# Key rows of a block in the order own 64, next 32, and a new listed order of all engines

## The chip, the cores and the metric

The kernel runs on one core of a Trainium2 chip. The metric is the time of one execution in microseconds, as the device reports it; for each version the median of several runs is given. The span of a profile runs from the first to the last instruction and is a little shorter than that time.

## The reference

Block-sparse attention with a window, then a two-layer network. Four batches, eight heads, 768 positions, head size 64.

```python
# attention: block, window = 32, 16
k_sum = k.reshape(B, H, nb, block, D).max(axis=3)          # 24 block keys
v_sum = v.reshape(B, H, nb, block, D).mean(axis=3)         # 24 block values
scores_l = scale * (q @ k.T), kept where |i - j| < 16
scores_s = scale * (q @ k_sum.T) + log(32)
a = softmax(concat[scores_l, scores_s])                    # over 768 + 24 columns
attn = a @ concat[v, v_sum]
# network on x = attn as [3072, 512]
h = x @ w_in                                               # 512 -> 2048
out = (h * clip(h + 3, 0, 6) / 6) @ w_out                  # 2048 -> 512
```

## The kernel before

**Attention.** A batch's 768 queries are cut into 12 blocks of 64, shifted by 16 rows against the blocks of keys. A block of queries needs 96 key rows (`WIN`) and the 24 block maxima, so that a block's scores are one product of 120 rows (`KEYS`). `kaug[p]` holds the keys so arranged for pair p of heads, `vaug[i]` the values (batch b in `vaug[b % 2]`). Of the 96 rows of block t, rows 0 to 31 are the last 32 of block t - 1 and rows 32 to 95 the 64 of block t itself. The first block wraps around; a mask kills what does not belong. The queries of block t start 16 rows before 64 t, so the query tile `qT` begins with 16 wrapped rows.

Values arrive by `load_v` in rows 32 to 95; the rows of the block before are copied on the chip (`halo`, batches 0 and 1) or loaded a second time (`load_ahead` and the copy "round", batches 2 and 3). The block sums of the values (`vsum_first`, `vsum`) are products with an indicator `ind` over all 96 rows, in which the first 32 rows of the indicator are zero. Those rows must hold numbers, so `empty` fills them with zeros once for each of two tiles and four pairs, and halos and sums wait for that.

Each batch is worked off in two halves of six blocks. Half 0 is the upper half of the positions (`low(x)` is `(1 - x) * HQ`), because block 0 is the one that wraps around. A half of a batch is one stage s of the network, s = 0 to 7.

**Steps of attention, by tag.** `k`p transposes the keys of batch 0 and takes maxima, `q`g transposes queries, `w`bp turns keys and queries of batches 1 to 3 by block transposes on VectorE, `s`bph makes scores, exponentials (ScalarE) and masks (VectorE), `u`g makes block sums and spreads them, `v`bhg multiplies by values, divides by the sum and transposes to x. For s of 4 and above x is transposed by a VectorE block transpose and 16 small moves in SyncE's queue (line 649).

**The network.** F`s`x`ft` is one group of four matmuls into a bank of PSUM (line 667), a ScalarE relu (line 671) and a VectorE gate (line 672). G`s``ts`x0 accumulates 16 matmuls of 512 columns in four parts (line 684), then an output copy on ScalarE or VectorE (line 242) and a store in SyncE's queue. Of the last output tile three column slices are separate; one of them (`ofinish`, lines 698 and 699) is copied and stored by ScalarE.

**What sets the order.** The string `ORDER` lists every step; each engine executes its steps in the order of that list. `:A` and `:D` place a step that either ScalarE or VectorE can do. Dependences become waits. Buffers of PSUM (three banks "h", one "o", two pairs "S") are given out in the order of the list, the one longest free first, so that the list also fixes which step a bank waits for. Tokens such as `_40`, `-15` and `~12` are matmuls on a constant tile: 40 of 64 columns, 15 of 128, 12 of 512; `=3` is one of 192. All loads are issued by GpSimd: K, Q, V, H for keys, queries, values and next rows, I and O for the two weights. The list begins:

```python
c.0 K00.0 c.7 c.17 c.6 c.8:A K01.0 c.10:D c.5 c.1 _40 -15 k0.0 k0.2:A c.18 ~1 =2 k1.0 K02.0 ~12 =3 k2.0 k3.0 ...
```

Here `c.0` to `c.20` are the constants (`c.1` identity, `c.2` the window, `c.3` the bias, `c.4` the mask, `c.5` the indicator, `c.6` and `c.7` edges of `vaug`, `c.8` to `c.15` the zero fills, `c.17` to `c.20` edges of `kaug`). Keys of pair 0 are loaded first, those of pairs 2 and 3 (`K02`) together and last; then queries, values of pairs 0 to 3, and the wide query tiles `Q0w0` to `Q0w2` of the second half.

Of the kernel before, what the change touches and what calls it, by code (L numbers as in the profile page):

```python
# [9 lines left out]
F32 = mybir.dt.float32  # L10
BF16 = mybir.dt.bfloat16
AF = mybir.ActivationFunctionType
# [17 lines left out]
c.0 K00.0 c.7 c.17 c.6 c.8:A K01.0 c.10:D c.5 c.1 _40 -15 k0.0 k0.2:A c.18 ~1 =2 k1.0 K02.0 ~12 =3 k2.0 k3.0 c.15:D c.2 c.3  # L30
s000.0 k0.3:A c.13:D c.4 c.11:A k1.1 Q00.0 q0.0 k1.4 k0.1 c.20 k1.2:A Q01.0 ~2 =5 q1.0 k0.4 k1.3:D c.9:A c.14:A c.19 k2.3:A
q0.1:A s000.1 q0.2:A =1 s010.0 s010.1 k2.2:A k3.2:D k3.3:D k3.1 V00.0 h000.0:D h001.0:D k2.1 k2.4 s000.2 ~2 =5 v00.0 V01.0 u0.0
h010.0:D s020.0 c.16 s010.2 q1.2:A u0.3:D u0.1:D u0.4:D v01.0 v01.1 v01.2 v00.1 q1.1:A V02.0 h020.0:A h021.0:A h011.0:A v00.2
s020.1 v01.3 v00.3 V03.0 u1.0 u1.3:A h030.0:D s030.0 k3.4 ~2 s030.1 u1.4:D v01.4 h031.0:D Q0w0.0 Q0w1.0 v01.5:D Q0w2.0 =1 q3.0
q3.1:D q2.0 u1.1:A u1.2:D s020.2 v02.0 v02.1 v02.2 s021.0 v02.3 s030.2 v03.0 v03.1 q2.1:A v03.2 s011.0 v03.3 v00.4 v00.5:D
v02.4 s021.1 s011.1 s021.2 v03.4 v03.5:D s011.2 v02.5:A s031.0 s031.1 s001.0 s031.2 I2.0 F0x3.0 F0x3.1 F0x3.2 F0x3.3 F0x3.4
F0x3.5 I4.0 F0x6.0 F0x6.1 F0x6.2 F0x4.0 F0x4.1 F0x4.2 F0x4.3 v411.0 v411.1 F0x5.0 F0x4.4 F0x4.5 v411.2 s001.1 I8.0 u0.2:A
s001.2 F0x8.0 F0x8.1 F0x8.2 F0x5.1 I0.0 F0x5.2 F0x11.0 F0x1.0 F0x11.1 F0x11.2 F0x1.1 F0x1.2 F0x1.3 F0x1.4 F0x1.5 v410.0 v410.1
F0x7.0 F0x7.1 F0x7.2 v410.2 F0x10.0 F0x10.1 I12.0 F0x13.0 F0x13.1 F0x15.0 F0x15.1 F0x13.2 F0x10.2 v411.3 v411.4:D v410.3
v410.4:A F0x15.2 F0x14.0 F0x14.1 F0x14.2 F0x9.0 F0x9.1 F0x9.2 F0x0.0 F0x0.1 F0x2.0 F0x2.1 K13.0 K10.0 c.12:A F0x0.2 K12.0 K11.0  # L40
w10.0 Q1w1.0 F1x14.0 F1x14.1 F1x14.2 F1x4.0 F1x4.1 F1x4.2 F1x2.0 F1x2.1 F1x2.2 w10.1:D F0x2.2 F0x2.3 F0x2.4 F0x12.0 F0x12.1
F0x12.2 F1x8.0 F1x8.1 F1x8.2 F1x1.0 F1x1.1 F1x1.2 F0x0.3 F0x0.4 F0x0.5 F0x2.5 F1x9.0 F1x9.1 F1x9.2 F1x5.0 F1x5.1 F1x5.2 F1x15.0
F1x15.1 w11.0 w11.2 F1x15.2 w11.3:D Q1w4.0 Q1w2.0 Q1w0.0 w10.2 w10.3:D q6.0 q6.1:A q7.0 q7.1:A F1x7.0 F1x7.1 w11.1:A F1x7.2
F1x12.0 F1x12.1 F1x12.2 O0.0 G02x0.0 Q1w5.0 Q1w3.0 q4.0 q4.1:A q5.0 q5.1:A F1x6.0 F1x6.1 F1x6.2 O1.0 G02x0.1 s100.0 s100.1
s100.3 F1x3.0 w12.0 F1x11.0 F1x11.1 w13.0 w13.2 F1x3.1 F1x11.2 w12.2 w12.1:D O2.0 G02x0.2 s101.0 s101.1 O3.0 F1x10.0 G02x0.3
G02x0.4:A w13.3:D w13.1:A s101.3 F1x0.0 G00x0.0 G00x0.1 w12.3:D s100.2 s101.2 s100.4 V10.0 h100.0:D F1x10.1 h110.0:A F1x10.2
F1x3.2 s110.0 s110.1 s110.2 s101.4 s110.3 G00x0.2 G00x0.3 G00x0.4:A V12.0 u4.0 h130.0:D h120.0:A F1x0.1 u4.1:D u4.2:A u4.4:D
u4.3:D u4.5:D G02x0.5 G01x0.0 G01x0.1 G01x0.2 s110.4 F1x0.2 h111.0:A v100.0 v100.1 v100.2 h121.0:A v101.0 v101.1 v101.2 G01x0.3
G01x0.4:A K20.0 K21.0 K22.0 K30.0 K23.0 w21.0 F1x13.0 F1x13.1 F1x13.2 v100.3 v100.4:A w20.0 w21.3 G12x0.0 w21.2:A v101.3
v101.4:A V22.0 H2.0 h101.0:A w20.3 G12x0.1 G12x0.2 F2x2.0 F2x2.1 F2x11.0 F2x2.2 F2x11.1 F2x11.2 s111.0 w23.0 s111.3 F2x1.0  # L50
F2x1.1 F2x1.2 F2x3.0 F2x3.1 F2x3.2 F2x15.0 F2x15.1 F2x15.2 Q22.0 w23.3 G12x0.3 s111.1 G12x0.4:A F2x5.0 F2x5.1 h131.0:A F2x5.2
F2x6.0 G10x0.0 s111.2 w22.0 w22.3 s111.4 w23.4:A V20.0 H2.1:A K33.0 F2x13.0 F2x13.1 F2x13.2 G10x0.1 F2x6.1 F2x0.0 F2x0.1 F2x0.2
u5.0 u5.1:A u5.5:A F2x6.2 v110.0 v111.0 v111.1 v111.2 Q30.0 F2x4.0 F2x4.1 F2x4.2 Q21.0 Q23.0 Q20.0 w22.4:A F2x10.0 F2x10.1
# [109 lines left out]
def kernel(  # L163
# [80 lines left out]
    def low(x):  # L244

        return (1 - x) * HQ
# [563 lines left out]
```

## Time and profile before

| | |
|---|---|
| median of 3 runs | 216.65 us (216.47 to 217.7) |
| profiled execution: span from first to last instruction | 214.9 us |
| outside that span, median less span | 1.75 us |
| TensorE busy | 208.8 us, 97% |
| VectorE busy | 162.7 us, 76% |
| ScalarE busy | 135.9 us, 63% |
| GpSimd busy | 49.5 us, 23% |
| DMA moved | 22.68 MB |

The page gives no other time for the profiled execution than its span; the rest of its time lies before the first and after the last instruction. Engines: PE is TensorE, PEld its weight loads, DVE VectorE, ACT ScalarE, POOL GpSimd, SP SyncE. In the table of stretches a row gives from:to, the length, each engine's busy time with its instructions in brackets, the granted TensorE clock and the DMA share. In groups of instructions "busy, mean ns" stands ahead of the bar and the idle time of the engine before them behind it. A row of the chain gives its start, its length and what ran. Durations of one engine overlap, so that starts of two neighbours can lie closer than the duration of the first.

### The profile page before, as it was taken

What the parts mean: (1) busy time and instruction counts of PE and PEld (TensorE: products, weight loads), DVE (VectorE), ACT (ScalarE), POOL (GpSimd) and SP (SyncE); (2) the same over time, 40 slices, a digit from 0 to 9 for tenths busy, and PEclk for the clock granted to TensorE, in tenths of its full rate; (3) what the DMA queues carried; (4) which work ended last, traced back from release to release, by engine and by line L of the source; (5) the groups of instructions that cost most, each with busy time, mean ns of one, the idle gap of its engine ahead of it and who ended that gap; (6) DMA issues with size and microseconds to landing.
All of it is one profiled execution on the core that took longest, in us unless ns stands there. A gap on an engine that the chain in (4) does not pass through costs nothing.

```text
span 214.9 us, 6125 instructions
## 1 busy us (share of the span) xinstructions
PE 208.8 (97%) x2564; PEld 119.7 (56%) x2564; DVE 162.7 (76%) x318; ACT 135.9 (63%) x264; POOL 49.5 (23%) x66
## 2 busy tenths in 40 slices
PE   7998999999999999999999999999999999999994
PEld 7566656555555565565555555555555555564443
DVE  6987999999899999898899889887865555550021
ACT  3987878887898988756578696566346355520110
POOL 7977358906643244000000000000000000000000
PEclk9999999999999999999999999999999999999999
DMA  5999999999999999930334234113314400113123
GB/s 75 159 155 189 203 188 170 190 203 162 206 160 187 181 135 151 108 146 11 38 37 143 28 37 110 49 21 39 70 19 81 78 0 3 49 49 122 52 80 139
DMA packets 91724, 22.68 MB, mean 106 GB/s; under 512 B 82224, under 2 KB 88752, under 8 KB 91696
## 3 DMA queue, kind: packets, MB, share of 16 engines
q0 software_dynamic: 62288, 14.41, 72.7%
q1 hardware_dynamic: 29264, 7.80, 15.4%
q8 instruction: 20, 0.33, 0.6%
q10 hardware_dynamic: 144, 0.07, 0.1%
q14 instruction: 8, 0.07, 0.1%
HBM read 28.82 MB, written 6.29 MB: 163 GB/s over the span
## 4 chain that ended last, share of the span: by engine, by line
PE 86%; POOL 5%; DMA 4%; DVE 1%; ACT 1%; issue 1%; POOLq 0%
PE h L667 38%; PE o L684 33%; PE h L684 5%; DMA qwide<-in_q_dram 4%; PE S L624 3%; PE S L513 3%; POOL vaug L344 2%; PE S L554 1%; ACT vaug L242 1%; POOL first L306 1%; PE S L637 1%; POOL qwide L326 1%; PE S L440 1%; PE S L667 1%; POOL first L313 1%; PE h L582 1%
## 5 line engine op out<-in xcount | busy, mean ns | idle before, releaser
L667 PE MATMUL h<-x,win 128*128 128x384 bf16 x500 | 91.1, 326 | 0.3 <-DVE g L672 0.3
L671 ACT ACTIVATE r<-h 128x384 f32<-128x384 f32 x125 | 58.7, 492 | 38.8 <-PE h L667 36.8
L672 DVE SCALAR_TENSOR_TENSOR g<-r,h 128x384 bf16<-128x384 f32 x125 | 65.7, 546 | 22.7 <-ACT r L671 20.1
L684 PE MATMUL o<-wout,g 128*128 128x512 bf16 x336 | 81.7, 379 | 0.0
L667 PEld LDWEIGHTS <-win 128*128 128x128 bf16 x512 | 48.7, 98 | 35.9 <-issue 0.5
L684 PEld LDWEIGHTS <-g 128*128 128x128 bf16 x416 | 38.7, 98 | 37.4 <-issue 0.3
L521 ACT ACTIVATE at<-S 120x768 bf16<-120x768 f32 x24 | 18.6, 811 | 5.5 <-PE S L513 5.4
L242 ACT COPY ot<-o 128x512 f32<-128x512 f32 x17 | 10.0, 586 | 15.4 <-PE o L684 14.2
L522 DVE TENSOR_TENSOR at<-at,mask 96x768 bf16<-96x768 bf16 x24 | 12.6, 549 | 2.0 <-ACT at L521 1.6
L606 DVE TENSOR_TENSOR xn<-S,rc 128x768 bf16<-128x768 f32 x14 | 13.3, 950 | 0.3
L242 DVE COPY ot<-h 128x512 f32<-128x512 f32 (+1 forms) x3 | 1.6, 555 | 14.3 <-PE h L684 14.3
L344 POOL DMA_DIRECT2D vaug<-in_v_dram x10 | 11.8, 1191 | 0.4 <-DMA first<-in_k_dram 0.2
L684 PE MATMUL h<-wout,g 128*128 128x128 bf16 (+2 forms) x80 | 11.4, 294 | 0.0
L468 DVE TENSOR_REDUCE red<-kaug 128x24 bf16<-128x768 bf16 x12 | 11.2, 942 | 0.1
L242 ACT COPY vaug<-vaug 32x640 bf16<-32x640 bf16 (+3 forms) x17 | 8.9, 574 | 0.8 <-DMA vaug<-in_v_dram 0.5
L242 ACT COPY vaug<-vs 24x1536 bf16<-24x1536 bf16 x6 | 8.8, 1468 | 0.6 <-DVE vs L242 0.5
L456 DVE STREAM_TRANSPOSE kaug<-kraw 128x768 bf16<-128x768 bf16 x8 | 8.1, 1020 | 0.3 <-PE S L513 0.3
L778 PE MATMUL o<-idle 128*128 128x64 bf16 (+2 forms) x70 | 7.0, 278 | 1.1 <-DVE idle L288 1.1
L334 POOL DMA_DIRECT2D kraw<-in_k_dram x8 | 5.9, 737 | 8.9 <-DVE kaug L456 7.3
L513 PEld LDWEIGHTS <-kaug 32*128 32x128 bf16 x576 | 5.3, 92 | 4.4 <-issue 3.6
L643 DVE STREAM_TRANSPOSE y<-xn 128x768 bf16<-128x768 bf16 x8 | 7.6, 964 | 0.2
L624 PEld LDWEIGHTS <-at 120*64 120x64 bf16 x336 | 6.2, 111 | 2.6 <-issue 1.5
(107 smaller groups left out, 183.6 us busy)
## 6 DMA issues: line engine op xcount, KB each, us to landing
out_dram<-ot SPq DMA_DIRECT2D x19, 256.0 KB, 2.3
vaug<-in_v_dram POOLq DMA_DIRECT2D x6, 384.0 KB, 13.1
wout<-in_moe_w_out_dram POOLq DMA_DIRECT2D x4, 512.0 KB, 9.9
win<-in_moe_w_in_dram POOLq DMA_DIRECT2D x3, 512.0 KB, 10.8
kraw<-in_k_dram POOLq DMA_DIRECT2D x8, 192.0 KB, 12.9
x<-y SPq DMA_DIRECT2D x64, 24.0 KB, 2.0
first<-in_k_dram POOLq DMA_DIRECT2D x6, 192.0 KB, 12.3
first<-in_q_dram POOLq DMA_DIRECT2D x6, 192.0 KB, 12.3
```

Of the source, the lines that this page charges most:

```text
L242: {"ACT": nc.scalar.copy, "DVE": nc.vector.tensor_copy, "POOL": nc.gpsimd.tensor_copy}[eng](o, i)
L344: op("POOL", "dma128", lambda: nc.gpsimd.dma_start(out=o[BLK:WIN, a:z, 0:D], in_=rows[:, a:z]), w=[("v", b % 2, c) for c in range(lo, hi)] ...
L468: op("DVE", "max", lambda: nc.vector.tensor_reduce(red.slot[:], w[:, :, BLK:WIN].rearrange("p t (n c) -> p t n c", n=2), axis=AX.X, op=ALU ...
L513: nc.tensor.matmul(X[g // 2].slot[:, g % 2, i * QB:(i + 1) * QB], kaug[2 * u + m][rows, t], qT[rows, 2 * u + m, t * QB:(t + 1) * QB], star ...
L521: op("ACT", "exp", lambda a=a, e=e: nc.scalar.activation(a, X[e].slot[0:KEYS, :, 0:HALF], AF.Exp, scale=scl), r=[X[e]], w=[("at", p, half)])
L522: op("DVE", "masking", lambda m=m: nc.vector.tensor_tensor(m, m, mask[:, low(half):low(half) + HQ].unsqueeze(1).to_broadcast([WIN, 2, HQ, ...
L606: nc.vector.tensor_tensor(o, src[..., 0:D], r.unsqueeze(len(r.shape)).to_broadcast(list(o.shape)), op=ALU.mult)
L624: nc.tensor.matmul(X.slot[64 * c:64 * c + 64, i, m:m + D + 1], a[:, t * QB:(t + 1) * QB], vaug[b % 2][0:KEYS, h, t, 0:D + 1], start=True, ...
L667: nc.tensor.matmul(bank(h)[:, 0:HALF], w_in_sb[:, kt, cols], xt[s].slot[:, kt], start=(kt == 0), stop=(kt == NP - 1))
L671: op("ACT", "relu", lambda: nc.scalar.activation(r.slot[:], bank(h)[:, 0:HALF], AF.Relu, bias=0.5, scale=1.0 / 6.0), r=[h], w=[r])
L672: op("DVE", "gate", lambda: nc.vector.scalar_tensor_tensor(gt[s].slot[:, ft], r.slot[:], 1.0, bank(h)[:, 0:HALF], op0=ALU.min, op1=ALU.mul ...
L684: nc.tensor.matmul(o.slot[:, a:z], gt[s].slot[:, ft, ts * 128:(ts + 1) * 128], w_out_sb[:, ft, a:z], start=(ft == 0), stop=(ft == NFT - 1))
```

## The change

Key rows of block t are now its own 64 in rows 0 to 63 and the first 32 of block t + 1 in rows 64 to 95; the last block wraps around. The queries of block t start at 64 t + 16, and the 16 wrapped rows stand at the end of `qT`. Half 0 is the lower half of the positions. The block sums read rows 0 to 63 alone, so their indicator has 64 rows, the eight zero fills are gone, and neither halos nor sums wait for them or for the neighbouring rows. Wrapped stores and loads move from the first to the last tile. The list is new as a whole: its opening loads `K02` first, then both query loads, `K01`, `K00` and values 3, 2, 1, 0, and begins TensorE with 17 constant matmuls of 512 columns and 17 of 128.

```diff
-c.0 K00.0 c.7 c.17 c.6 c.8:A K01.0 c.10:D c.5 c.1 _40 -15 k0.0 k0.2:A c.18 ~1 =2 k1.0 K02.0 ~12 =3 k2.0 k3.0 c.15:D c.2 c.3
-s000.0 k0.3:A c.13:D c.4 c.11:A k1.1 Q00.0 q0.0 k1.4 k0.1 c.20 k1.2:A Q01.0 ~2 =5 q1.0 k0.4 k1.3:D c.9:A c.14:A c.19 k2.3:A
+c.0 c.6 K02.0 Q01.0 Q00.0 c.1 K01.0 ~17 -17 k2.0 K00.0 V03.0 c.9 c.12 c.10 V02.0 k3.0 k3.3:A c.11 k2.1 c.2 ~5 =2 q0.0 q1.0
+V01.0 k2.4 k3.1 k3.2:D V00.0 q0.1:D c.3 Q0w2.0 k2.2:A k3.4 ~3 s030.0 q0.2:A c.4 k0.0 q1.2:A s030.1 c.5 k2.3:A s020.0 q1.1:A
+s020.1 k1.0 h030.0:D Q0w1.0 s030.2 v03.0 k0.2:A s020.2 k1.2:A k0.1 k1.1 c.8 Q0w0.0 u1.0 k0.4 s000.0 I4.0 k1.4 I2.0 I0.0 s000.1
+u1.3:D k1.3:D u1.1:D s000.2 s010.0 h020.0:D k0.3:D h000.0:A s010.1 v03.1 u0.0 v00.0 h010.0:D v03.2 v02.0 u0.1:D v02.1 u0.3:A
+s010.2 v00.1 v03.3 v01.0 I12.0 I8.0 v02.2 v01.1 u1.2:A q3.0 q2.0 h011.0:A v00.2 v00.3 v02.3 v01.2 v00.4 K13.0 u1.4:D q3.1:D
+h031.0:A q2.1:D v01.3 v00.5:D s021.0 s001.0 v03.4 c.7 h021.0:A v02.4 v01.4 s021.1 s031.0 v03.5:D K10.0 v02.5:D F0x4.0 s001.1
+v01.5:A s021.2 K12.0 s011.0 F0x3.0 F0x3.1 F0x3.2 s031.1 K11.0 s011.1 s001.2 F0x6.0 F0x3.3 F0x1.0 Q1w1.0 F0x3.4 F0x1.1 F0x6.1
...
+F4x2.0 F4x10.1 G32x0.1 G32x0.2 F4x2.1 F4x10.2 G32x0.3 w30.2:D v211.2 F4x11.0 G32x0.4:A F4x0.2 s300.0 s300.3 v210.3 F4x3.0
+F4x2.2 G30x0.0 F4x3.1 u6.5:D G30x0.1 F4x11.1 s300.1 v211.3 s300.4 G30x0.2 u6.2:A w30.5:A w32.1 G01x0.5 F4x3.2 F4x1.0 w33.5:D
...
-G70x0.4:D G70x0.5 G60x0.0 G60x0.1 G60x0.2 G72x0.4:D G72x0.5 G60x0.3 G71x256.1 G71x256.2 G60x0.4:D G60x0.5 G71x256.3 G71x256.4
-G71x384.0 G71x384.1 G71x384.2 G71x384.3 G71x384.4:D G71x384.5
+G52x0.5 G70x0.2 G72x0.3 G71x0.0 G70x0.3 G71x0.1 G72x0.4:D G61x0.5 G72x0.5 G71x256.0 G60x0.2 G60x0.3 G71x384.5 G71x0.2 G70x0.4:A
+G71x256.1 G71x0.3 G60x0.4:D G71x0.4:D G71x256.2 G71x256.3 G71x256.4 G60x0.5 G70x0.5 G71x0.5
...
-    ind = sb([WIN, NQ, 32], BF16, "ind")
+    ind = sb([QB, NQ, 32], BF16, "ind")
...
-        return (1 - x) * HQ
+        return x * HQ
...
-    def empty(eng, i, c):
...
-        for c in range(NP):
-            op(EITHER, "empty", lambda eng, i=i, c=c: empty(eng, i, c), r=["idle"], w=[("vh", i, c)])
...
-        op("POOL", "dma128", lambda: nc.gpsimd.dma_start(out=o[BLK:WIN, a:z, 0:D], in_=rows[:, a:z]),
+        op("POOL", "dma128", lambda: nc.gpsimd.dma_start(out=o[0:QB, a:z, 0:D], in_=rows[:, a:z]),
...
-            copy(eng, o[0:BLK, hs, a:z, 0:D], o[QB:WIN, hs, a - 1:z - 1, 0:D])
+            copy(eng, o[QB:WIN, hs, a:z, 0:D], o[0:BLK, hs, a + 1:z + 1, 0:D])
...
-            out=w[:, :, BLK:WIN].rearrange("p t (r s) -> p t s r", s=2), in_=blocks_of(kraw[(b + 1) % 2][:])),
+            out=w[:, :, 0:QB].rearrange("p t (r s) -> p t s r", s=2), in_=blocks_of(kraw[(b + 1) % 2][:])),
...
-                    nc.tensor.matmul(T.slot[32 * c:32 * c + 32, 0, 0:2 * D], ind[:, t], vaug[i][0:WIN, 2 * c:2 * c + 2, t, 0:D],
+                    nc.tensor.matmul(T.slot[32 * c:32 * c + 32, 0, 0:2 * D], ind[:, t], vaug[i][0:QB, 2 * c:2 * c + 2, t, 0:D],
                                      start=(t == 0), stop=(t == NQ - 1))
-        op("PE", "sums4", mms, r=[("v", i, c) for c in range(NP)] + ([("vh", i, c) for c in range(NP)] if b == 1 else [("vh", i)]) + ["ind"], w=[T])
+        op("PE", "sums4", mms, r=[("v", i, c) for c in range(NP)] + ["ind"], w=[T])
...
-            b, row = s // 2, 128 * ((s % 2 * 3 + ts + 3) % 6) - PAD
-            n = max(-row, 0)
+            b, row = s // 2, 128 * (s % 2 * 3 + ts) + PAD
+            n = max(row + 128 - S, 0)
```

179 lines of the change are left out of this document (83 added, 96 removed).

## The prediction

> **What bounds the kernel now.** I read the page first, then the table of stretches, then the chain that ended last.
>
> ```profile
> span 214.9 us, 6125 instructions
> ```
> ```profile
> core 0: us, PE busy (x) PEld busy (x) DVE busy (x) ACT busy (x) POOL busy (x), PEclk, DMA share, GB/s
> 8.00:16.00 8.00, 7.79 (x156) 4.74 (x155) 6.98 (x22) 6.93 (x14) 6.92 (x9) 1.00 2.13 161
> 24.00:44.00 20.00, 19.70 (x228) 12.12 (x220) 18.70 (x38) 16.43 (x32) 13.32 (x16) 1.00 1.68 187
> 44.00:64.00 20.00, 19.87 (x371) 10.80 (x369) 18.60 (x37) 16.94 (x31) 9.31 (x10) 1.00 1.97 182
> 64.00:84.00 20.00, 20.00 (x251) 11.62 (x249) 19.01 (x31) 17.69 (x39) 8.26 (x9) 1.00 1.85 164
> 84.00:104.00 20.00, 20.00 (x291) 11.17 (x290) 18.46 (x33) 13.13 (x27) 0.00 (x0) 1.00 0.83 90
> 104.00:124.00 20.00, 20.00 (x237) 10.79 (x235) 17.73 (x33) 14.61 (x26) 0.00 (x0) 1.00 0.34 63
> ```
> ```profile
> 20.31 0.73 PE h L442 x10
> ...
> 24.24 2.06 PE h L667 x12
> ...
> 57.50 0.84 PE S L554 x48
> ...
> 119.52 1.73 PE o L684 x8
> 121.25 1.95 PE h L667 x12
> ...
> 210.36 1.58 PE h L684 x28
> ```
>
> From 24.2 us on TensorE has hardly a gap (19.70 and 19.87 of 20, then all of it) until its last matmul at 210.36 + 1.58 = 211.9. An F matmul costs 1.95/12 = 0.162 us, a G matmul 1.73/8 = 0.216 us, and the change alters the number of neither. So a new order can win only in the opening before 24.2 us and in the 3.0 us after 211.9; in the 187.7 us between it can only lose. Next to TensorE stands VectorE: 18.70 + 18.60 + 19.01 + 18.46 + 17.73 = 92.5 of the 100 us from 24 to 124. That is the second limit.
>
> **The parts that cost nothing.**
>
> ```profile
> L283 DVE MEMSET vaug<- 32x768 f32 x3 | 2.1, 698 | 0.4 <-issue 0.2
> L285 ACT ACTIVATE vaug<-idle 32x768 f32<-32x768 bf16 x5 | 4.1, 836 | 0.0
> L554 PE MATMUL S<-vaug,ind 96*32 96x128 bf16 x144 | 2.6, 220 | 0.0
> L513 PE MATMUL S<-qT,kaug 32*128 32x64 bf16 x576 | 6.6, 190 | 0.0
> L490 PE MATMUL S<-qT,kaug 64*128 64x64 bf16 x96 | 2.6, 191 | 0.1
> ```
> ```profile
> 2.42 0.70 DVE L283 MEMSET vaug<- 32x768 f32 x1 [0.19 <-issue]
> ...
> 4.84 0.26 DVE L262 TENSOR_SCALAR bias<-band 96x384 bf16<-96x384 bf16 x1 [0.25 <-POOL band L258]
> 5.19 0.70 DVE L283 MEMSET vaug<- 32x768 f32 x1
> 5.82 0.44 DVE L265 COPY mask<-band 96x768 bf16<-96x768 bf16 x1
> ...
> 6.63 0.96 DVE L403 TENSOR_REDUCE red<-h 128x24 bf16<-128x768 bf16 x1
> ```
>
> The eight zero fills go: 3 x 0.70 us of VectorE and 5 x 0.84 us of ScalarE. VectorE's three lie between 2.42 and 5.89, before its first reduction over keys at 6.63: it would wait for keys anyway. Four of ScalarE's five lie in the opening, where it is busy 6.93 of 8 us, and it has 11 to 34% free in every later stretch. Gain 0; its bounds are 0 and the 2.1 us of VectorE. The block sums read 64 rows and not 96 with the same five groups of matmuls (5 x 0.84 = 4.2 us). If rows set the time, a third (1.4 us) would go; but matmuls of 64 and of 32 rows take 191 and 190 ns, so I take 0. Their wait for the next-block rows goes as well; TensorE was not idle there. Wrap-around rows, their split stores and split loads move to the other end in equal number: 0.
>
> **The opening, in the new order.** Key pairs 2 and 3 come first in one load of 384 KB, then both query loads, then keys 1 and 0, then v in the order 3, 2, 1, 0.
>
> ```profile
> 1.13 3.71 PE L778 MATMUL o<-idle 128*128 128x64 bf16 x55 [1.13 <-DVE idle L288]
> ...
> 6.45 2.85 PE L778 MATMUL o<-idle 128*128 128x512 bf16 x13
> ```
> ```profile
> first<-in_k_dram POOLq DMA_DIRECT2D x1, 384.0 KB, 5.5
> ```
> ```profile
> 25.56 1.20 DVE L672 SCALAR_TENSOR_TENSOR g<-r,h 128x384 bf16<-128x384 f32 x2
> ...
> 28.92 1.48 DVE L672 SCALAR_TENSOR_TENSOR g<-r,h 128x384 bf16<-128x384 f32 x3
> ```
>
> The filler matmuls show two speeds: 40 of 64 and 15 of 128 columns, 4480 in 3.69 us, are 0.82 ns a column; thirteen of 512, 6656 in about 2.8, are 0.42. The new filler ahead of the first transpose is 17 x 512 + 17 x 128 = 10880 columns from the same 1.13 us: 4480 slow until 4.8, the other 6400 x 0.42 = 2.7 until 7.5. The 384 KB need 5.5 us from issue at 1.36, so 6.9. The first transposes (0.5 us) thus start at 7.5, and VectorE's first reduction at 8.0, where it is 6.63 now.
>
> From there to the end of its first gate (line 672, due at 25.56 + 0.55 = 26.1 now) VectorE has 40 instructions now and 43 in the new order. Counted with the mean of each kind, that is 17.9 and 20.6 us: bias (0.26), mask (0.44 and its small fills), block indicator and one edge fill, 2.1 us together, which now fill its wait for keys, come after the keys, and one masking, two query copies and a sum copy are added (1.9), against two halo copies, a spread and two fills fewer (1.3). Durations overlap: three gates of 0.546 take 1.48, a ratio of 0.90; with the waits between engines I take 0.93. So 8.0 + 20.6 x 0.93 = 27.2: the first gate is 1.1 us late. Up to the gate of F0x15 follow 12 gates, two reciprocals, two scalings, a copy and a transpose, 10.5 x 0.93 = 9.8, until 37.0 us. By then TensorE has run as many F groups as by the same time before (16 of s = 0 but one, two of s = 1), because before it was itself the limit, at 0.65 us a group. Walked on bank by bank, the first block sum of batch 1 starts near 56.5, now 57.50, with 0.9 us more matmuls behind it. I take 0 for the opening, between -1.5 (VectorE at ratio 0.86) and +1.6.
>
> **VectorE after the opening.** The order hands copies from ScalarE to VectorE: nine of twelve spreads of block sums (now six), ten output copies (now seven), three wide query copies (now one); two third-row copies and two spreads of maxima go the other way.
>
> ```profile
> L672 DVE SCALAR_TENSOR_TENSOR g<-r,h 128x384 bf16<-128x384 f32 x125 | 65.7, 546 | 22.7 <-ACT r L671 20.1
> L522 DVE TENSOR_TENSOR at<-at,mask 96x768 bf16<-96x768 bf16 x24 | 12.6, 549 | 2.0 <-ACT at L521 1.6
> L606 DVE TENSOR_TENSOR xn<-S,rc 128x768 bf16<-128x768 f32 x14 | 13.3, 950 | 0.3
> L468 DVE TENSOR_REDUCE red<-kaug 128x24 bf16<-128x768 bf16 x12 | 11.2, 942 | 0.1
> L456 DVE STREAM_TRANSPOSE kaug<-kraw 128x768 bf16<-128x768 bf16 x8 | 8.1, 1020 | 0.3 <-PE S L513 0.3
> ```
>
> F4x6 reuses the bank that the gate of F4x13 frees. From 8.0 to that gate stand 71 gates (39), 22 maskings (12), 20 transposes of k and q (20), 12 reductions (11), 10 scalings (10) and 78 smaller ones (36): 128 us of durations, x 0.90 = 115.3 of busy time. Behind F4x6 TensorE still has 220 F, 240 G and 192 attention matmuls, 83.5 us. To end at 211.9 as now, VectorE must be through by 128.4, busy 115.3 of 120.4 us, 96%. Its best stretch now is 19.01 of 20, 95%, its mean 92.5%. At 95% the gate comes at 129.4: +1.0 us. I take +1.0, between 0 and +4.3.
>
> [...]
>
> **SyncE's queue.**
>
> ```profile
> 118.51 10.53 SPq L649 DMA_DIRECT2D x<-y  x16
> ```
> ```profile
> 136.87 1.31 PE L667 MATMUL h<-x,win 128*128 128x384 bf16 x7
> ```
>
> The x of s = 4 to 7 goes through 16 moves in SyncE's in-order queue, 10.5 us. Now s = 5 starts them at 118.5 and its first F at 136.9, 7.8 us after the last issue. In the new order the last scaling and transpose of s = 5 stand behind two F4 gates on VectorE, near 124, the moves end near 135, and F5x0 is due at 211.9 - 76.7 (its remainder) = 135.2. Between 0 and +2; as a late VectorE delays both sides alike I take +0.2.
>
> **The tail.**
>
> ```profile
> 211.11 0.27 ACT L698 COPY ot<-h 128x128 f32<-128x128 f32 x1 [5.26 <-PE h L684]
> 211.96 0.29 DVE L242 COPY ot<-h 128x128 f32<-128x128 f32 x1 [0.82 <-PE h L684]
> ```
> ```profile
> out_dram<-ot ACTq DMA_DIRECT2D x1, 64.0 KB, 2.1
> out_dram<-ot SPq DMA_DIRECT2D x1, 64.0 KB, 1.6
> ```
>
> Now VectorE copies the last 128 columns (0.29) and SyncE stores them (1.6). In the new order the last is the slice that ScalarE copies and stores itself: 0.27 + 2.1. Half a us later: +0.5, between 0 and +1.
>
> **The sum.** 0 + 1.0 + 0.2 + 0.5 = +1.7 us on a span of 214.9. The median of the runs, 216.65, is 1.75 above that span; 216.65 + 1.7 = 218.3 us, 0.8% more. A measurement here tells about 1% (2.2 us) from no change.
>
> **Rivals.** (1) *VectorE becomes the bound.* Below 96% busy from 8 to 128 us every percent costs 1.3 us; at today's 92.5% the gate falls at 8.0 + 124.7 = 132.7 and the end 4.3 later: with the tail 221.5. For it: some 10 us less work on ScalarE and none less on VectorE, and setup moved into its busy time. Against: it idles now because TensorE is late for it, and would be fuller as the bound.
> (2) *The opening gains.* At ratio 0.86 the first gate ends at 25.7, the first F comes up to 1.5 us earlier and the later losses fail: 215.1. Against: the v loads need the same bytes as now, and TensorE's q3 waits for the wide query loads (20.3 now) as before.
> (3) *The slow clock lasts longer.* If the second speed came one such spell (3.4 us) later, the filler would end 1.7 us later, with every VectorE step behind it: 220.0. Against: TensorE starts to be busy at the same 1.13.
> [...]
>
> **Chances.** Forecast 0.50, of which 0.06 reaches over 218.8; rival 1 0.28; rival 2 0.15, of which 0.07 lies under 214.5; rival 3 0.07. That makes faster 0.07, same 0.44 + 0.08 = 0.52, slower 0.06 + 0.28 + 0.07 = 0.41. The forecast's own range is 216 to 219.5; with the rivals 214.9 to 222.
>
> **What would show it.** Right: first F matmul at 24 to 25 us, first gate ended near 27, VectorE at 19 of 20 us or more up to 124, gaps on TensorE between 24 and 130 of 1 to 2 us in all, ended by VectorE, last matmul near 213. Wrong: first F under 23, VectorE idle over 1 us in a stretch while TensorE is full, a gap at F5x0 over 2 us, or ScalarE ahead of line 667 in the waits.

## The result, and the profile after

The changed kernel takes 223.97 us (median of 4 runs, 222.75 to 224.71), the kernel before 216.8 on the same chip: ratio 1.0326, 95% interval 1.0285 to 1.0367. The forecast was 218.3, with 222 as the upper end. The profiled execution is the longest of the four (224.71), 0.7 us over the median. Ratios here leave out executions in which the clock was disturbed for longer than in the quickest ones of the same kernel.

The page and its row of granted clocks, 40 slices of 5.6 us:

```profile
span 223.0 us, 6046 instructions
PE 213.9 (96%) x2527; PEld 120.5 (54%) x2527; DVE 162.2 (73%) x316; ACT 126.0 (56%) x257; POOL 49.1 (22%) x66
PEclk9998579999999999999999999999999999999999
```

The span grew by 8.1 us, VectorE's work not at all (162.7 before). TensorE's busy time grew by 5 us, and the digits 8, 5, 7 say where: from 20.72 to 30.96 us its clock was halved (the last section has the rows). The opening on TensorE and VectorE, in the view in order of time (start, length, what, count, and in brackets the idle time before and what ended it):

```profile
1.13 7.71 PE L768 MATMUL o<-idle 128*128 128x512 bf16 x34 [1.13 <-DVE idle L279]
8.77 0.87 PE L382 MATMUL h<-ident,first 96*64 96x96 bf16 x32
...
18.80 0.35 PE L480 MATMUL S<-qT,kaug 64*128 64x64 bf16 x12 [1.81 <-DVE kaug L398]
...
29.94 0.82 PE L657 MATMUL h<-x,win 128*128 128x384 bf16 x2
```
```profile
9.34 0.96 DVE L393 TENSOR_REDUCE red<-h 128x24 bf16<-128x768 bf16 x1 [7.44 <-PE h L382]
...
15.92 0.96 DVE L393 TENSOR_REDUCE red<-h 128x24 bf16<-128x768 bf16 x1 [1.27 <-ACT kaug L241]
...
32.45 1.02 DVE L662 SCALAR_TENSOR_TENSOR g<-r,h 128x384 bf16<-128x384 f32 x2 [0.49 <-ACT r L661]
```

The first reduction over keys starts at 9.34 (before 6.63), the F matmuls come at 29 to 30 (24.17), the first gate starts at 32.45 (25.56). By then 6.9 us are lost. Counted as start of the first F matmul plus TensorE's work behind it at full clock, 6.0 us of that remain; 1.4 come between there and the last matmul, and 0.7 behind it (3.65 us from the last matmul to the end, 2.95 before). Most of the 1.4 is still the halved clock. In the changed kernel from the first F matmul to the clock's rise and on to the last matmul, and in the kernel before from the first F matmul to the last (length; TensorE's busy time first; clock behind the last bracket):

```profile
29.07:30.96 1.89, 1.89 (x21) 0.97 (x18) 1.82 (x5) 1.75 (x3) 0.62 (x1) 0.50 1.81 188
30.96:219.37 188.41, 187.61 (x2113) 103.95 (x2111) 142.93 (x260) 109.17 (x225) 27.65 (x32) 1.00 0.77 90
```
```profile
24.17:211.92 187.75, 187.32 (x2122) 104.47 (x2116) 142.70 (x257) 117.88 (x231) 30.72 (x35) 1.00 0.82 99
```

TensorE works 1.89 us at half clock, which loses 0.95 us, and stands idle for 0.80 us behind that, against 0.43 in the kernel before: 0.4 us more.

The stretches behind the opening, as before (length; busy time of each engine with its instructions; clock):

```profile
44.00:64.00 20.00, 20.00 (x376) 11.27 (x374) 19.05 (x36) 16.59 (x37) 9.67 (x12) 1.00 2.10 173
64.00:84.00 20.00, 19.97 (x286) 11.21 (x284) 18.98 (x31) 16.57 (x36) 6.25 (x7) 1.00 1.46 144
84.00:104.00 20.00, 19.65 (x278) 10.96 (x279) 19.36 (x38) 13.08 (x27) 1.56 (x3) 1.00 1.05 97
104.00:124.00 20.00, 20.00 (x277) 11.11 (x262) 19.41 (x35) 10.94 (x25) 0.00 (x0) 1.00 0.35 74
124.00:144.00 20.00, 20.00 (x241) 10.82 (x240) 14.97 (x31) 13.53 (x25) 0.00 (x0) 1.00 0.28 48
```

Up to 124 us VectorE is 95 to 97% busy, the height that the prediction named; TensorE still has hardly a gap. So the body, the work behind the first F matmul, is tight and nearly unhurt, and the loss lies in the first 33 us. That stretch, from the first key reduction to the first gate's start, is the yardstick of what follows. In the kernel before and in the changed one:

```profile
6.63:25.56 18.93, 17.66 (x368) 11.53 (x367) 16.44 (x46) 15.95 (x30) 13.95 (x18) 1.00 1.77 179
```
```profile
9.34:32.45 23.11, 19.56 (x389) 13.55 (x384) 19.37 (x51) 15.75 (x32) 14.53 (x19) 0.78 1.84 182
```

18.93 us became 23.11. VectorE has 2.9 us more to do in it and stands idle for 3.7 us, not 2.5; the clock is 0.78 on average.

### The profile page after: what moved, and what is told of

Same layout as the page of the kernel before. It is cut to its first block, busy times and chain, and to the rows that moved or that the text cites. A ratio compares the mean times of both kernels' runs of the same rounds, so it can differ in the third digit from the quotient of the medians.

```text
span 223.0 us, 6046 instructions
## 1 busy us (share of the span) xinstructions
PE 213.9 (96%) x2527; PEld 120.5 (54%) x2527; DVE 162.2 (73%) x316; ACT 126.0 (56%) x257; POOL 49.1 (22%) x66
## 4 chain that ended last, share of the span: by engine, by line
PE 81%; DVE 9%; ACT 7%; issue 1%; DVEq 0%
PE h L657 35%; PE o L674 29%; PE h L674 4%; PE o L768 3%; PE S L503 2%; PE S L614 2%; ACT r L661 1%; DVE red L393 1%; ACT vaug L241 1%; DVE g L662 1%; DVE kaug L241 1%; DVE vaug L241 1%; ACT at L486 1%; ACT kaug L241 1%; DVE red L458 1%
## 5 line engine op out<-in xcount | busy, mean ns | idle before, releaser
L657 PE MATMUL h<-x,win 128*128 128x384 bf16 x500 | 93.5, 328 | 0.2
L661 ACT ACTIVATE r<-h 128x384 f32<-128x384 f32 x125 | 59.4, 493 | 46.4 <-PE h L657 44.8
L511 ACT ACTIVATE at<-S 120x768 bf16<-120x768 f32 x24 | 19.4, 815 | 2.6 <-PE S L503 2.5
L241 ACT COPY ot<-o 128x512 f32<-128x512 f32 x14 | 8.2, 586 | 9.8 <-PE o L674 9.7
L674 PE MATMUL h<-wout,g 128*128 128x512 bf16 (+2 forms) x80 | 11.4, 294 | 0.0
L241 DVE COPY ot<-o 128x512 f32<-128x512 f32 x7 | 4.8, 690 | 8.6 <-PE o L674 8.6
L768 PE MATMUL o<-idle 128*128 128x512 bf16 (+1 forms) x40 | 9.0, 395 | 1.1 <-DVE idle L279 1.1
L393 DVE TENSOR_REDUCE red<-h 128x24 bf16<-128x768 bf16 x3 | 2.8, 935 | 8.7 <-PE h L382 7.4
L486 ACT ACTIVATE at<-S 120x768 bf16<-120x768 f32 x8 | 6.6, 832 | 2.1 <-PE S L480 2.1
L241 ACT COPY ot<-h 128x512 f32<-128x512 f32 x1 | 0.6, 586 | 12.5 <-PE h L674 12.5
```

The costliest lines, as they stand in the source:

```text
L241: {"ACT": nc.scalar.copy, "DVE": nc.vector.tensor_copy, "POOL": nc.gpsimd.tensor_copy}[eng](o, i)
L511: op("ACT", "exp", lambda a=a, e=e: nc.scalar.activation(a, X[e].slot[0:KEYS, :, 0:HALF], AF.Exp, scale=scl), r=[X[e]], w=[("at", p, half)])
L657: nc.tensor.matmul(bank(h)[:, 0:HALF], w_in_sb[:, kt, cols], xt[s].slot[:, kt], start=(kt == 0), stop=(kt == NP - 1))
L661: op("ACT", "relu", lambda: nc.scalar.activation(r.slot[:], bank(h)[:, 0:HALF], AF.Relu, bias=0.5, scale=1.0 / 6.0), r=[h], w=[r])
L674: nc.tensor.matmul(o.slot[:, a:z], gt[s].slot[:, ft, ts * 128:(ts + 1) * 128], w_out_sb[:, ft, a:z], start=(ft == 0), stop=(ft == NFT - 1))
L768: nc.tensor.matmul(o[:, 0:c * 64].rearrange("p (c x) -> p c x", c=c), idle[:], idle[:, 0:64].unsqueeze(1).to_broadcast([128, c, 64]), star ...
```

## The experiments

### Which half of the change, and which part of the list

Four kernels: the new layout under the old list (names translated); the old list up to the first F and the new one behind; the reverse; and the new list with its small setup put where VectorE waits for keys.

```diff
# layout alone: the whole ORDER
-c.0 c.6 K02.0 Q01.0 Q00.0 c.1 K01.0 ~17 -17 k2.0 ...
+c.0 K00.0 c.7 c.9 c.6 K01.0 c.5 c.1 _40 -15 k0.0 ...
# setup
-... V02.0 k3.0 k3.3:A c.11 k2.1 c.2 ~5 ... q0.1:D c.3 ... c.4 ... c.5 ... c.8 ... c.7
+... K00.0 c.2 ... c.10 c.11 c.3 c.4 c.5 c.8 c.7 V02.0 k3.0 k3.3:A k2.1 ~5 ...
```

> The changed kernel's code with its row layout (own 64 rows, then 32 of the next block, no zero fills, block sums from 64 rows), but the list of all engines in the order of the kernel before, with only the names of rows and banks translated. Theory O (the listed order, above all of the opening, costs the 7 us): 216 to 217.5 us, as before; first F matmul at 24 to 25 us, granted clock 1.00 to the end. Theory L (the layout itself costs): 219 us or more. Theory B (VectorE bounds the body from 24 to 128 us, whatever the opening does): 216 to 217.5 too, since the old list also has the old shares of VectorE and ScalarE.

Measured: 218.03 us, ratio 1.0033 (0.9993 to 1.0072). As long as the clock holds, the layout is free, and with it the missing fills and the shorter sums: neither a gain nor a loss that can be told. But the clock holds less often: three of the ten executions had a mean clock of 0.967 to 0.984 and took 220.5 to 222.0 us, while none of the thirteen of the kernel before was under 0.992.

> The changed kernel with the old list up to the first F matmul and the new list behind it. Theory O: the opening is worth 6.0 us and the rest 1.4 + 0.7, so about 218.9 us, between 218 and 219.8; first F matmul near 24.2 us. Theory L: 222 or more. Theory B: the body is bound by VectorE and an earlier start is lost again as gaps of TensorE from 24 to 128 us: 221 to 223.

Measured: ratio 1.0108 (1.0012 to 1.0203), 219.3 us; the median of all four executions is 221.87, because two of them had a mean clock of 0.969 and took 223.8 and 224.1, the other two (0.989 and 0.997) 219.9 and 219.3. These two lie at the upper edge of what theory O has; with two executions the interval is wide. The profile is of one of the former, with half clock from 18.07 us for 13.65 us:

```profile
14.66:18.07 3.41, 2.68 (x77) 1.84 (x76) 3.13 (x10) 1.86 (x4) 1.78 (x3) 1.00 3.26 145
18.07:21.48 3.41, 3.02 (x29) 1.65 (x30) 2.28 (x7) 2.58 (x7) 2.78 (x4) 0.50 1.43 199
```

> The mirror image: the changed kernel with the new list up to the first F matmul and the old list behind it. Theory O: 216.8 + 6.0 = 222.8 us, between 221.8 and 223.8, with the first F near 29 us and a stretch of half clock before it. Theory L: like the kernel with the layout alone, 219 or more, but no later than it by over 2 us. Theory B: 217 to 218.5, as the old rest gives VectorE's slack back.

Measured: 222.61 us, ratio 1.0235 (1.0164 to 1.0307), half clock for 10.24 us in the profile. Theory O holds: the new opening alone carries most of the loss. The old rest is worth 1.4 us behind it by the medians (223.97 less 222.61), and the intervals of the two ratios overlap. Of these 1.4 us 0.65 are the tail: 2.98 us from the last matmul to the end here.

> The changed kernel with one thing undone in its list: the small setup (window on GpSimd behind the first key work; bias, masks, block indicator and edge fills of VectorE ahead of the first key reduction, in the time in which VectorE waits for keys). Theory O in the form that VectorE's queue is late because the setup stands behind the keys: TensorE's gap of 1.81 us at 17 us closes, the clock isn't halved, and the time is 2 to 4 us under the changed kernel, 220 to 222 us. Rival (the filler's late end alone makes the opening late): within 1 us of the changed kernel, 223 to 224.5, the gap and the half clock staying.

Measured: 224.2 us, ratio 1.0315 (1.0253 to 1.0378). A miss for this form of the theory: the setup was hidden, TensorE still paused for 1.42 us between 16 and 20 us, the clock was halved all the same (0.52 from 20 to 24 us, 0.50 from 24 to 28), and nothing came back. Where 1.8 us of setup stand is not the cause.

### The clock

Between the first query transposes and the first F the old list has seven filler tokens, the new one a single one. Two kernels put fillers into the new list (at one place, the `~7` below, then at all four), one took the seven out of the kernel before, one had the four and also the old start filler and the setup hidden.

```diff
# one place / all four
-... q0.2 ... ~3 s030.0 ... I0.0 s000.1 ... v03.2 v02.0 ... v03.3 v01.0
+... q0.2 ... ~6 s030.0 ... I0.0 ~7 s000.1 ... v03.2 ~2 v02.0 ... v03.3 ~2 v01.0
# the kernel before without them
-... Q01.0 ~2 =5 q1.0 ... q0.2:A =1 s010.0 ... s000.2 ~2 =5 v00.0 ... k3.4 ~2 s030.1 ... Q0w2.0 =1 q3.0
+... Q01.0 q1.0 ... q0.2:A s010.0 ... s000.2 v00.0 ... k3.4 s030.1 ... Q0w2.0 q3.0
```

> The changed kernel with seven filler matmuls of 512 columns (about 1.5 us) put into its list in front of the first score matmuls of batch 0, where TensorE stands idle for 1.81 us. Theory C (the pauses of TensorE in the first 13.65 us of full clock bring the 10.24 us of half clock, and these are the larger part of the loss): no half clock, first gate near 29 us, not 33, and 219.5 to 221 us; if one pause less is not enough for the clock (0.71, 0.44 and 0.59 us stay open), as the changed kernel. Theory V (VectorE's later queue alone sets the opening, the clock is a by-product): within 1 us of the changed kernel even at full clock.

Measured: 222.92 us, ratio 1.0297 (1.0256 to 1.0339); half clock still for 6.8 us (0.85 on average from 7.84 to 30.20 us). The median is 1.0 us under the changed kernel, but the intervals of the two ratios overlap.

> The kernel before, with its order, layout and fills, but without the seven groups of filler matmuls that its list has between the first query transposes and the first F matmul (the new list has one such group there). Theory C: the clock is halved for 10 to 14 us from about 18 us on, and the time rises by 4 to 5 us to 221 to 222. Theory V: the fillers stand in waits and nothing waits for them, so 216.5 to 217.5 as before.

Measured: the ten executions lie between 215.98 and 223.4 us, median 219.98, against 216.04 to 218.59 with the fillers. Two of them had full clock and took 216.0 and 216.4; the other eight had a mean clock of 0.961 to 0.984. The profiled one (span 216.9):

```profile
13.24:16.65 3.41, 2.97 (x82) 2.25 (x80) 2.94 (x10) 2.94 (x6) 2.24 (x3) 1.00 2.38 152
16.65:20.07 3.42, 3.24 (x53) 2.19 (x53) 2.61 (x9) 2.64 (x8) 3.06 (x4) 0.50 1.83 183
```

The ratio, which rests on the three quickest executions, is 1.0007 (0.9953 to 1.006): what differs is how often the clock falls. The fillers do no work that is used, yet without them the clock falls in eight of ten executions, and these take 2 to 7 us more than the other two. In this kernel they hold the clock.

> The changed kernel with filler matmuls in all four pauses of TensorE between 12 and 24 us (3, 7, 2 and 2 matmuls of 512 columns more). Theory C: clock 1.00 from its rise on, as in the kernel before, and 219 to 220.5 us. Theory V: 223 to 224.5 us.

Measured: 222.65 us, ratio 1.0277 (1.0249 to 1.0306), clock 1.00 through the opening. Theory C, in which the clock was the larger part, falls: the held clock gives back 1.3 us at most. The intervals of the two ratios still overlap a little, and the one execution of this kernel with a mean clock of 0.982 took 222.6 us, no more than the one at 1.00 (222.7). The yardstick:

```profile
8.21:30.31 22.10, 20.04 (x409) 12.75 (x403) 18.90 (x51) 15.84 (x32) 14.08 (x18) 1.00 2.11 178
```

22.10 us at full clock, where the old order needs 18.93.

> The same fillers, and in addition the narrow start filler of the kernel before (40 of 64 and 15 of 128 columns, then 10 of 512, in place of 17 of 128 and 17 of 512) and the small setup of VectorE ahead of its first key reduction. Theory C: full clock, and the opening's other 1.5 us come back with the earlier start: 217.5 to 219 us, first key reduction at 7.5 to 8 us. Theory V: the setup and the start are the larger part, so 218 to 219.5 here while the kernel with the fillers alone stays at 223.

Measured: 223.21 us, ratio 1.0297 (1.0257 to 1.0337): a miss for both theories. VectorE has 1.8 us less to do in the stretch and the stretch isn't shorter:

```profile
8.69:31.57 22.88, 19.70 (x374) 12.44 (x374) 17.06 (x41) 14.97 (x29) 14.77 (x20) 0.93 1.77 183
```

The clock fell late in this stretch (0.93 on average), but the two executions at 0.999 and 1.000 took 222.3 and 222.6 us, as with the fillers alone. So VectorE's sum of work doesn't set it either; VectorE is busy for 75% of it.

### The start, the heads of the queues, the tail, the engines

The start filler alone as in the kernel before (`_40 -15 ~10` for `~17 -17`):

> The changed kernel with the narrow start filler of the kernel before alone (40 matmuls of 64 columns, 15 of 128, 10 of 512) in place of 17 of 128 and 17 of 512. If the wide filler at the slow clock is what makes the first key reduction late (9.34 us in its profile, between 8.2 and 9.4 in the others): first reduction near 7.5 us, first gate 1 to 1.5 us earlier, 222.5 to 223 us, clock still halved. Rival (the chain behind doesn't hang on it): 223.5 to 224.5.

Measured: 223.12 us, ratio 1.0274 (1.0228 to 1.0321), first reduction at 8.17 and clock halved (0.78 on average from 8.17 to 31.65 us): up to 0.9 us, inside the spread of the runs.

In the kernel with all pauses filled, the chain that ended last goes back and forth between the engines. A part of it (start, length, engine, tile and line):

```profile
19.82 0.89 DVE kaug L241 x3
...
21.35 0.31 DVE vf L241
...
21.68 0.26 ACT vf L241
...
21.96 0.82 ACT at L486
...
22.82 0.65 PE o L572 x21
```

ScalarE's queue at that place:

```profile
18.98 0.83 ACT L241 COPY vaug<-vaug 32x768 bf16<-32x768 bf16 x1
21.68 0.26 ACT L241 CAST vf<-o 24x128 bf16<-24x128 f32 x1 [1.87 <-DVE vf L241]
21.96 0.81 ACT L486 ACTIVATE at<-S 120x768 bf16<-120x768 f32 x1
```

The exp at 21.96 has had its scores since 18.8; it stands behind a copy that waits for VectorE, which stands behind key copies. I put both such places right:

```diff
-k0.1 k1.1 c.8 Q0w0.0 u1.0 k0.4 ... u0.1:D v02.1 u0.3:A s010.2
+k0.1 k0.4 k1.1 c.8 Q0w0.0 u1.0 ... u0.1:D v02.1 s010.2 u0.3:A
```

> The changed kernel with the fillers of the run with all pauses filled, and two places of the list set otherwise: VectorE's spread of the maxima of key pair 0 straight behind their reduction (before the reduction of pair 1), and on ScalarE the second exp of batch 0 ahead of the copy of u0 that waits 1.87 us for VectorE. Theory Q (the opening is set by instructions that wait at the head of VectorE's and ScalarE's queues for one another): first gate 0.5 to 1 us earlier than 30.85, 221.6 to 222.2 us. Rival V (VectorE's sum of work from 16 us on sets the gate, which waits elsewhere don't shorten): within 0.4 us of 222.65.

Measured: 223.13 us, ratio 1.0276 (1.0238 to 1.0314), as without the edit. A miss for theory Q in this form, as far as it goes: the exp began at 20.52, not 21.96, and VectorE waited elsewhere. But in four of the six executions the clock fell for a step (0.991); the other two took 221.3 and 222.4 us, against 222.5 to 222.8 without the edit, so that a gain of some 0.7 us can't be excluded.

> The changed kernel with its list, but behind the first F matmul every copy and spread on the engine (VectorE or ScalarE) that it has in the kernel before: 34 tokens change their suffix, none its place. Theory B (VectorE, at 95 to 97% from 44 to 124 us, costs the 1.4 us of the body): VectorE falls to 93% there and the time to 222.4 to 223.2 us. Rival (the body's loss is in the order itself, or in single waits for a bank): 223.6 to 224.6 us.

Measured: 225.27 us, ratio 1.0393 (1.0356 to 1.0429), 1.3 us over the changed kernel (the intervals just touch), and no faster in any case. VectorE did fall:

```profile
44.00:64.00 20.00, 19.64 (x373) 10.74 (x362) 18.27 (x38) 16.53 (x30) 9.06 (x10) 1.00 2.00 180
104.00:124.00 20.00, 19.99 (x237) 10.78 (x235) 18.10 (x35) 12.13 (x25) 0.00 (x0) 1.00 0.33 72
124.00:144.00 20.00, 18.73 (x234) 10.18 (x233) 12.85 (x25) 15.82 (x27) 0.00 (x0) 1.00 0.28 48
```

Compared at the same steps, TensorE in this profile was 2.4 us ahead of the changed kernel at F1x4 (near 40 us) and 2.3 at F3x12 (near 111): the relief of VectorE moved nothing. By 144 us 1.7 of the lead were gone, with a pause of TensorE of 1.27 us for a gate. The spread of block sums that VectorE copies in 0.56 us in the changed kernel takes ScalarE 1.47 us here; the relu behind it comes late, and VectorE's gate waits for it 2.42 us, not 0.80. In the changed kernel, then in this one:

```profile
126.87 0.56 DVE L241 COPY vaug<-vs 24x1536 bf16<-24x1536 bf16 x1
...
132.41 1.02 DVE L662 SCALAR_TENSOR_TENSOR g<-r,h 128x384 bf16<-128x384 f32 x2 [0.80 <-ACT r L661]
```
```profile
127.09 1.47 ACT L241 COPY vaug<-vs 24x1536 bf16<-24x1536 bf16 x1
```
```profile
131.90 1.02 DVE L662 SCALAR_TENSOR_TENSOR g<-r,h 128x384 bf16<-128x384 f32 x2 [2.42 <-ACT r L661]
```

The body isn't bound by VectorE's fullness; at this place the new list is better off with the spread on VectorE.

> The changed kernel with the last output tile's third slice (128 columns, copied by VectorE and stored by SyncE) put last, as in the kernel before, and the slice that ScalarE copies and stores before it. If the tail's 0.7 us are that copy and store: 3.0 us from the last matmul to the end, not 3.65, and 223.2 to 223.5 us. If the stores of other slices set the end: 3.6 us, and 223.8 to 224.2.

Measured: 222.5 us, ratio 1.0246 (1.0217 to 1.0275). From the last matmul (218.90) to the end (222.1) it takes 3.2 us, so 0.4 of the 0.7 are the last copy and store. The median is 1.5 us under the changed kernel; the other 1.1 us aren't explained by the edit.

### The opening with keys first

Most steps of key pairs 0 and 1 go ahead of the products with the bias, the scores and the exps of pairs 3 and 2; three setup operations fill VectorE's wait; the start filler is narrow:

```diff
-... k3.4 ~3 s030.0 q0.2:A c.4 k0.0 q1.2:A s030.1 c.5 k2.3:A s020.0 q1.1:A s020.1 k1.0 h030.0:D Q0w1.0 s030.2 v03.0 k0.2:A s020.2 k1.2:A k0.1 k1.1
+... k3.4 q0.2:A ~2 k0.0 s030.0 q1.2:A k0.2:A k0.1 k0.4 s030.1 k2.3:A k1.0 s020.0 q1.1:A s020.1 h030.0:D Q0w1.0 k1.2:A s030.2 v03.0 s020.2 k1.1
```

> The same, and in addition: narrow start filler, three setup operations (bias, mask, block indicator, 1.8 us) in VectorE's wait for keys, and the transposes, copies and reductions of key pairs 0 and 1 moved ahead of the covers, scores and exps of pairs 3 and 2 in the queues of TensorE, ScalarE and VectorE. Theory Q: VectorE's wait of 1.1 to 1.4 us for these copies goes, its 1.8 us of setup are hidden, so the first gate ends at 27 to 28 us and the time is 219 to 220.2 us. Rival (the order in which keys and values are loaded sets the opening): first gate at 30 or later, 222 to 223 us.

Measured: 223.21 us, ratio 1.0294 (1.0264 to 1.0323). The run says little, because its seven fillers before s000.1 fell into half clock and stood on the chain for 2.5 us. Without them:

> The run with key pairs 0 and 1 ahead of the scores, with one filler matmul of 512 columns in place of the seven in front of the first score matmuls of batch 0 (in that run these seven took 2.46 us at half clock on the chain of waits, with VectorE idle for 3.1 us behind them) and without the two pairs of fillers behind. Theory Q (the opening is set by the order in the queues of TensorE, ScalarE and VectorE): first gate near 28.5 us, not 31.2, and 219.5 to 221 us. Rival (order of loads, or VectorE's sum of work): 222.5 us or more.

Measured: 223.24 us, ratio 1.03 (1.0241 to 1.036): a miss. The clock fell at 14.72 and TensorE itself became the chain (the block sums of u1 take 1.46 us here, 0.84 at full clock):

```profile
14.98 0.54 PE L572 MATMUL h<-vaug,at 96*64 96x65 bf16 x12 [0.91 <-ACT at L486]
15.45 1.46 PE L526 MATMUL h<-vaug,ind 64*32 64x128 bf16 x24
...
20.12 1.46 PE L526 MATMUL o<-vaug,ind 64*32 64x128 bf16 x24
```

The same opening with the old rest:

> The re-ordered opening of the first run of this call, with the old list behind the first F matmul. If the parts add up (the old rest was worth 1.4 us behind the new opening): 1.4 us under the first run, 218 to 219.6 us; rival (the new opening leaves the buffers in a state that costs the old rest its gain): equal to the first run.

Measured: 221.97 us, ratio 1.0238 (1.017 to 1.0307), with clocks of 0.968 to 0.977: again under the halved clock. Then with short fillers in the waits (`~4 k0.0`, `~1 s030.1`, `~1 s020.1`, `~4 v03.0`, `=1` before s000.1, v02.0 and v01.0), with the new rest and the old one:

> The re-ordered opening (key pairs 0 and 1 ahead of the scores) with short fillers in TensorE's waits between 10 and 15 us: 4 matmuls of 512 columns before the transposes of pair 0, 1 and 1 before the first two score groups, 4 before the first values, and single ones of 64 columns later. In the run without them the clock was halved from 14.72 us for 13.65 us and the chain of waits from 15 to 25 us went over TensorE. Theory Q plus the clock: clock 1.00 through the opening, first gate near 28.7 us, not 31.35, and 220 to 221.2 us. Rival (loads or VectorE's sum of work): 222.5 us or more although the clock stays full.

> The same opening with the old list behind the first F matmul. If the parts add up: 1.0 to 1.6 us under the other run of this call, 218.5 to 220 us, against 216.8 for the kernel before. If the clock is halved again: 221 to 222 us as in the earlier run of this pair.

Measured: 222.39 us, ratio 1.0269 (1.0235 to 1.0304), and 219.9 us, ratio 1.017 (1.0137 to 1.0203). The fillers held the clock until 23.7 and 22.4 us. It fell at the end of a step with a new pause of TensorE, which in the first of the two stands in the middle of a group of twelve equal matmuls and has no releaser:

```profile
20.71 0.28 PE L572 MATMUL h<-vf,at 24*64 24x65 bf16 x7 [0.24 <-DVE vf L241]
22.09 0.28 PE L572 MATMUL h<-vf,at 24*64 24x65 bf16 x5 [1.10 <-issue]
```

The yardsticks, new rest and old rest:

```profile
8.57:31.50 22.93, 20.66 (x399) 13.29 (x394) 17.96 (x45) 15.94 (x32) 15.06 (x20) 0.85 1.76 184
```
```profile
8.07:29.04 20.97, 19.45 (x385) 13.05 (x379) 17.37 (x46) 15.83 (x32) 14.40 (x18) 0.92 1.76 185
```

The yardstick isn't of the opening alone: the two lists are the same up to the first F matmul, and 0.7 of the 2.0 us between them fall ahead of it, 1.3 behind.

219.9 us is the best that I got out of the new opening, 4 us better than the change and 3 us behind the kernel before. No kernel here beats that one.

## Why the prediction was wrong

**The opening is the step that failed**: put at 0, between -1.5 and +1.6, it cost 6.0 us in the profile (whose execution is 0.7 us over the median). Its first gate was forecast for 27.2 and ended at 33.0. The 5.8 us between, by the steps of the working:

- *Start.* "VectorE's first reduction at 8.0" came at 9.34: 1.3 us. In the profile of the change the clock rose at 7.07 us, in that of the kernel before at 4.48, though both begin matmuls at 1.13: 5.94 us of slow clock against 3.35 (a filler matmul of 512 columns took 629 ns up to 7.0 us in the change, 381 ns from 4.5 us on in the kernel before). This is rival 3, which I gave 0.07; it put the rise 3.4 us later, and these two profiles are 2.59 us apart. The start filler, 17 matmuls of 512 columns and 17 of 128, takes 7.71 us in the changed kernel and ends at 8.84; the same filler ends at 7.70 us with all pauses filled and at 8.86 with the heads moved. In the profiles with this filler the first reduction came anywhere from 7.84 us (seven fillers at one place) to 9.36 (heads moved), so a part of this term is chance. Under the old start of the list it came at 6.63 us (before), 6.75 (old opening) and 7.30 (layout alone).
- *The factor 0.93.* Forecast were 20.6 us of durations in 19.2 us; from the first reduction to the gate's end it took 23.7, 4.5 more. This is the term that was mis-sized most. The factor came from three gates in a row (0.90), not from this stretch: in the old order the stretch from 6.63 to 26.1 us takes 19.5 us for the 17.9 that the prediction counts, a ratio of 1.09. So the forecast gave 2.7 us more work less time than the old order takes. At 1.09 the 20.6 us come to 22.4, the first gate ends at 30.4, and 3.2 of the 4.5 us are foreseen. That gives the size and not the mechanism: a list of durations with a factor assumes that VectorE is what sets the stretch, and with 1.8 us of VectorE's work taken out of it the stretch got no shorter. In the new order it is a chain that goes back and forth: keys to ScalarE's copies, to VectorE's reductions, to TensorE's scores, to ScalarE's exps. With VectorE's busy time anywhere from 17.1 to 19.4 us and the clock from 0.70 to 1.00, the stretch took 22.1 to 23.5 us in each kernel here that kept the new rest behind the new or the re-ordered opening.
- *The clock.* Of these 4.5 us, the run with the clock held gives back 1.0 in the stretch (22.10 for 23.11), and 1.3 at most in the time. The prediction had no term for it, though the fillers were in the diff that it read: it costed the start filler and not the seven fillers behind it, without which TensorE pauses for 1.81 us and then runs at half speed for 10.24.

About 3 us of the opening stay open (22.10 us with the clock held, against 18.93). Half of them lie between the first reduction and the first F matmul (19.16 against 17.54 us), half between that and the first gate (2.94 against 1.39). They aren't the layout, the setup's place, the clock or VectorE's sum, and no head of a queue that I moved brought back more than 0.7; they go with the old list up to the first F, which brings 219.3 us where the clock holds (two executions), 4.7 under the change. That it is the order of the whole chain is argued from the chain of waits and from the last pair, not shown by one edit.

**The body**: +1.0 forecast, from gaps of TensorE that VectorE ends. Of the 1.4 us that the profile shows there, 0.95 are the halved clock of the opening, and TensorE's pauses grew by 0.4 only. The old rest behind the new opening brings 1.4 us by the medians, 0.65 of them tail (2.5 behind the re-ordered opening with short fillers, tail included). VectorE's height was right (95 to 97%); that this is what costs isn't borne out, since relief brought nothing. Rival 1 thus named the right sign and not the cause.

**SyncE's queue**: forecast +0.2, between 0 and +2. TensorE is busy 20.00 of 20 us from 124 to 144, where F5x0 falls (141.9), so no wait showed. **The tail**: +0.5 forecast, 0.7 measured, of which 0.4 are the copy and store named. **The parts at nothing** (fills, sums of 64 rows, wraps) hold where the clock does: 1.0033.

The sum of the later parts, +1.7, is near the 2.1 us measured, but for the body that is luck, since most of its share is the clock; what stood under the forecast was an opening costed with a ratio from another stretch.

## What to carry to other kernels

Filler matmuls in an opening can be part of the clock and not decoration, as the seven here, without which it fell in eight of ten executions (0.961 to 0.984): before a list is changed, count TensorE's idle time per step of the clock (3.41 us in these profiles) in the old and the new order. A ratio of elapsed time to durations belongs to one stretch of one order: try it first on the old order, where this one would have shown 1.09 and not 0.93; for a new order, walk its chain across the engines from wait to wait. And undo halves first: two hybrid lists located the loss at once, while no single edit of the changed list brought back more than 1.5 us, and the one that did (the tail) explains only 0.4 of them.

## What the runs showed of the hardware

**Half clock after short pauses.** The changes of the clock read here lie 3.41 us or a multiple of it apart: in the changed kernel it rose at 7.07 us, was halved at 20.72 (13.65 us, 4 steps) and rose again at 30.96 (10.24 us, 3 steps). The changed kernel, cut at these steps (length; TensorE's busy time first; clock behind the last bracket):

```profile
10.48:13.90 3.42, 2.71 (x56) 1.54 (x54) 3.32 (x10) 1.68 (x4) 3.33 (x5) 1.00 2.44 156
13.90:17.31 3.41, 3.09 (x90) 2.07 (x84) 1.64 (x6) 3.23 (x8) 1.48 (x2) 1.00 2.83 149
17.31:20.72 3.41, 1.92 (x60) 1.49 (x62) 3.19 (x10) 1.51 (x2) 2.84 (x4) 1.00 1.42 199
20.72:24.14 3.42, 2.40 (x62) 1.89 (x58) 3.23 (x11) 1.37 (x4) 1.95 (x4) 0.50 1.37 202
27.55:30.96 3.41, 3.41 (x41) 2.19 (x39) 3.23 (x10) 3.27 (x5) 1.49 (x2) 0.50 1.72 186
30.96:34.37 3.41, 3.41 (x43) 2.08 (x42) 2.85 (x6) 2.36 (x6) 2.38 (x4) 1.00 2.15 164
```

A step in which TensorE stood idle for 1.49 of 3.41 us was followed by half clock, for three steps. In three other profiles a step at full clock with 1.34 us of idle TensorE (from 20.32 us, the re-ordered opening with short fillers and the new rest), 1.35 (from 24.36, fillers, start and setup together) and 1.40 (from 24.17, heads moved), as far as the records of matmuls go, was followed by it too. Of the steps with less, those with 0.73 us (from 14.66, the old opening with the new rest) and 0.44 (from 13.24, the kernel before without fillers) were followed by it; those with 1.11 (from 10.71, fillers, start and setup together), 0.87 (from 18.13, the kernel before) and 0.80 (from 21.84, all pauses filled) were not. Nor was the pause of 1.27 us between 124 and 144 us in the run with the engines of before: the clock stayed 1.00 to 144. Half clock lasted from one step (from 27.59, heads moved) to four (from 18.07, old opening). The longest single pause ahead of it in the changed kernel was 1.81 us; what counts besides idle time isn't settled.

**A pause inside a group of equal matmuls.** In four kernels (all pauses filled, heads moved, and the last pair) TensorE pauses inside a group of equal matmuls, and the view names "issue", no engine and no DMA, as what ended it: 0.33, 0.72, 1.10 and 1.01 us. In the first two it stands ahead of the last three matmuls of the group `o<-vf,at` (line 572), in the last pair ahead of the last five of a group `h<-vf,at` of twelve (same line). The layout alone has such a pause of 0.59 us elsewhere, inside a group of line 614, at 27.91 us. It isn't a wait that the list names, and what makes it isn't shown.
